# Output stores issued from ScalarE's queue in place of SyncE's, in a residual vector quantizer on one core

## The chip, the cores and the metric

The kernel runs on one core of a Trainium2 chip. The metric is device time in microseconds (us) of one execution, as a median over runs. The engines are named as in the profile: PE (TensorE, matrix products), PEld (its weight loads), DVE (VectorE), ACT (ScalarE), POOL (GpSimd) and SP (SyncE, which here only issues DMAs). "SPq" and "ACTq" are the instruction streams of SP and ACT where they issue DMAs.

## What is computed

The input `x` is 2 x 16000 x 512 in bf16. A three-tap depthwise convolution along time, then SiLU, then four stages of residual quantization with eight code words each, then a second three-tap depthwise convolution over the sum of the chosen words:

```python
z = silu(sum(xp[:, i:i+T, :] * dw_enc[i] for i in range(3)))
res, q = z, 0
for s in range(4):
    cb = codebooks[s]
    d2 = |res|^2 - 2 * res @ cb.T + |cb|^2
    sel = cb[d2.argmin(-1)]
    q = q + sel
    res = res - sel
y = sum(qp[:, i:i+T, :] * dw_dec[i] for i in range(3))
```

The output `y` has the shape and type of `x`, 32.8 MB.

## The kernel before

**Tiling.** The 32000 rows are laid out as 128 partitions by 250 groups. `SIZES` cuts the 250 groups into 17 chunks: 4, 12, fourteen of 16, and 10. Inside a chunk, channels go in four blocks of 128 (index `i`).

**One chunk.** `load` brings `x` in transposed, channels on partitions: for chunks from the third on, `one` (L395) issues one transposing DMA for each group and two for the edges, 18 for a chunk of 16, all on SP, into a tile `XT` of which there are two. `front` forms the convolution: DVE makes three products for each block (L449, tiles `Z` and `T`), of which the first one or two sums run as accumulating DMAs from POOL (L455) and the rest on DVE (L457). ACT does the exponential (L461), the addition of one (L466) and the reciprocal (L162), and DVE multiplies into `RES` (L476). `stage` runs four times: PE scores (L540, L545), DVE takes a maximum (L553, `TR`) and ACT moves the dot products out (L556, `PR`); DVE finds the nearest word in six small steps (L574 to L601); PE turns the one-hot marks (L611), ACT copies them (L618, `OHT`); PE pairs (L626), ACT copies (L631, `OHP`), PE gathers the chosen words (L653, `SEL`) and DVE adds them to `RES` (L659).

**The output.** `finish` calls `outputs` once for every four groups, 64 times in all. There, for each pair of groups, PE decodes into PSUM (L676, tile `Y`) and ACT copies into an SBUF tile `YSB` (L682, 128x1024). After the second pair, `store` (L686) issues one DMA of 512 KB from `YSB` to the output. There are two `YSB` tiles (`YB = 2`), so ACT's copies for the third set of four groups wait until the store of the first has landed.

**What sets the order.** Nothing is scheduled on the chip. `Plan` (L43 to L119) is a list scheduler that runs while the kernel is built: each piece of work is a task with an engine, a time for which it holds that engine, a time after which its result is there, what it needs, a due time, and buffers that it takes and gives (`XT`, `Z`, `T`, `E`, `Y`, PSUM banks and so on). `run` walks through modelled time, gives each free engine the ready task with the earliest due time, and emits its instructions at that moment. Each engine then runs its instructions strictly in the order of emission, and waits on semaphores. `Plan` has lanes that are no engines: the stores were tasks of a lane `OUT` (1.5 held, 3.0 to the result), beside the lane `SP` of the transposes (1.4 held, 2.2 to the result, each one after the one before). So the plan treated stores and transposes as independent of each other, though both were instructions of SP, in order of emission. When PE has nothing ready, `run` may insert a filler product (L350) that keeps its clock up.

**Semaphores of the DMAs.** The framework gives the DMAs of SP and ACT eight semaphores in turn. Each such DMA waits, before it is issued, until the DMA eight places earlier in the order of emission has landed, whichever of the two engines issued that one.

Of the kernel before, what the change touches and what calls it, by code (L numbers as in the profile page):

```python
# [13 lines left out]
ACT = mybir.ActivationFunctionType  # L14
# [108 lines left out]
def kernel(  # L123
# [8 lines left out]
    nc = tc.nc  # L132
# [12 lines left out]
    outv = out.flatten_outer_dims().rearrange("(p g) d -> p g d", g=S)  # L145
# [42 lines left out]
    for i in range(KT):  # L188
# [4 lines left out]
    plan = Plan({"XT": 2, "Z": ZB, "T": TB, "E": EB, "Y": YB, "psG": 2, "psA": 3, "RES": 3, "KEY": 3,  # L193
                 "OH": 3})
# [473 lines left out]
    def outputs(groups, needs, due):  # L668

        u = {}  # L670

        def decode(k):
            Y = u[k] = psA.tile([P, 2, D], F32, name="Y", tag="psa")
            for h, (_, terms) in enumerate(groups[k:k + 2]):
                for a, (lhs, rhs) in enumerate(terms):
                    nc.tensor.matmul(Y[:, h, :], lhsT=lhs(), rhs=rhs, start=(a == 0), stop=(a == len(terms) - 1))  # L676

        def pair(k):
            if k == 0:
                u["YSB"] = ypool.tile([P, J, D], out.dtype, name="YSB")  # L680
            n = len(groups[k:k + 2])
            nc.scalar.activation(u["YSB"][:, k:k + n, :], u[k][:, 0:n, :], ACT.Copy)  # L682

        def store():
            g = groups[0][0]
            nc.sync.dma_start(out=outv[:, g:g + len(groups), :], in_=u["YSB"][:, 0:len(groups), :])  # L686

        c = None
        for k in range(0, len(groups), 2):
            count = sum(len(t) for _, t in groups[k:k + 2])  # L690
            d = plan.add("PE", 0.22 * count, 0.22 * count + 0.2, needs, due, lambda k=k: decode(k), take=("psA",))
            c = plan.add("ACT", 0.93, 1.05, [c, d], due, lambda k=k: pair(k), take=("Y",) if k == 0 else (), give=("psA",))
        plan.add("OUT", 1.5, 3.0, [c], due, store, give=("Y",))

    def edge(name, src, shift):
        t = const.tile([P, P], BF16, name=name)
# [10 lines left out]
    def finish(st, due):  # L707
        A0, A1, A2, A3, B0, B3 = (DEC[k] for k in ("A0", "A1", "A2", "A3", "B0", "B3"))
        g0 = st["g0"]
        for m in range(st["MB"]):  # L710
            g = g0 + m * J
            cur = lambda m=m: st["OHT"][:, m, :]
            prev = kept.get("last")
            needs = [st["turned"], kept.get("turned")] + decoder
            todo = []
            if prev is None:
                FIRST = const.tile([P, P], BF16, name="FIRST")
                kept["first"] = plan.add("DVE", 0.2, 0.3, [st["turned"]], due, lambda cur=cur: nc.vector.tensor_copy(FIRST, cur()))
                kept["FIRST"] = lambda: FIRST
            else:  # L720
                todo.append((g - 1, [(prev, A3), (cur, B3)]))
                todo.append((g, [(cur, A0), (prev, B0)]))
            todo.append((g + 1, [(cur, A1)]))
            todo.append((g + 2, [(cur, A2)]))
            kept["last"] = cur
            if g + J < S:
                outputs(todo, needs, due + 0.02 * m * PERIOD)
                continue
            assert S - 1 == g + 1
            right = plan.add("DVE", 0.5, 0.7, [kept["first"]], due, edge("RIGHT", kept["FIRST"], 1))  # L730
            left = plan.add("DVE", 0.5, 0.7, [st["turned"]], due, edge("LEFT", cur, -1))
            todo[-2] = (S - 1, [(cur, A1), (lambda: kept["RIGHT"], B3)])
            outputs(todo[:-1], needs + [right], due)
            outputs([(0, [(kept["FIRST"], A0), (lambda: kept["LEFT"], DEC["A2LO"])])], needs + [left], due)
        kept["turned"] = st["turned"]
# [41 lines left out]
```

## Time and profile before

| | us |
|---|---|
| median of 3 runs (798.14 to 801.6) | 798.77 |
| time of the profiled execution | 797.84 |
| its span, first to last instruction | 796.1 |
| DVE busy | 672.9 |
| ACT busy | 575.3 |
| PE busy | 565.2 |

How to read it: the profile lists groups of instructions with their line, engine, operation, what they write and read, how many there are, their busy time and mean duration, and the idle time of the engine just before them with what ended it (the releaser). A second view lists waits as "engine line <- releaser: us in total, times, longest us". The queue that SP feeds carried 69.77 MB and took 42.9% of the 16 DMA engines' time, POOL's queue 47.63 MB and 34.6%, and ACT's queue 0.13 MB (three small loads at the start) and 0.1%. The transposes run from 2.5 us to 645 us of the span; 41 of the 64 stores are issued in that time and 23 behind it.

### The profile page before, as it was taken

How to read it: one execution, taken by the hardware profiler on the slowest of the kernel's cores; microseconds unless marked ns; L12 is line 12 of the kernel's file. 1: busy time of each engine (PE TensorE's matmuls, PEld its weight loads, DVE VectorE, ACT ScalarE, POOL GpSimd, SP SyncE). 2: the span in 40 equal slices, each digit the busy share in tenths (PEclk: the TensorE clock that was granted, in tenths of full speed). 3: DMA queues.
4: the chain of work that ended last, by engine and by line, in shares of the span. 5: the costliest groups of instructions: out<-in, count | busy, mean ns of one | idle time of the engine just before them, and what ended most of it. 6: DMA issues, size and time to landing. Idle time of an engine off the chain costs nothing. (4 is left out here: it accounts for less than half of the span.)

```text
span 796.1 us, 24168 instructions
## 1 busy us (share of the span) xinstructions
PE 565.2 (71%) x10688; PEld 323.2 (41%) x10751; DVE 672.9 (85%) x1249; ACT 575.3 (72%) x658; POOL 98.4 (12%) x116
## 2 busy tenths in 40 slices
PE   3036776667667677777786877777774887888885
PEld 3012443244433444343444444444532444454542
DVE  4899688988978998698978999999995999999851
ACT  1519763869489795779779597989684898777454
POOL 1301002010201101010110111011110121100000
PEclk9557799769899999899988999989997899999999
DMA  7614869795999998899996799899989864422133
GB/s 194 113 26 76 164 100 177 143 155 127 169 159 203 201 168 144 175 172 187 138 229 137 132 203 174 172 203 190 193 144 195 145 166 115 114 75 81 55 135 133
DMA packets 167571, 119.08 MB, mean 150 GB/s; under 512 B 146921, under 2 KB 147306, under 8 KB 167338
## 3 DMA queue, kind: packets, MB, share of 16 engines
q1 hardware_dynamic: 153252, 69.77, 42.9%
q0 software_dynamic: 14064, 47.63, 34.6%
q8 instruction: 84, 1.38, 0.7%
q14 instruction: 21, 0.17, 0.1%
q10 hardware_dynamic: 150, 0.13, 0.1%
HBM read 3.70 MB, written 32.77 MB: 46 GB/s over the span
## 5 line engine op out<-in xcount | busy, mean ns | idle before, releaser
L659 DVE TENSOR_TENSOR RES<-RES,SEL 128x2048 bf16<-128x2048 bf16 (+2 forms) x204 | 222.5, 1137 | 29.9 <-PE SEL L653 29.4
L545 PEld LDWEIGHTS <-RES 128*64 128x64 bf16 x8064 | 164.2, 117 | 113.6 <-issue 84.0
L545 PE MATMUL PS<-RES 128*64 128x80 bf16 (+1 forms) x8064 | 189.8, 207 | 21.1 <-DVE RES L476 11.3
L653 PE MATMUL SEL<-OHP,W 64*128 64x512 bf16 (+2 forms) x1224 | 159.3, 393 | 33.6 <-ACT OHP L631 12.6
L455 POOL DMA_DIRECT2D Z<-T x90 | 86.3, 973 | 579.2 <-ACT PR L556 83.4
L682 ACT ACTIVATE YSB<-Y 128x1024 bf16<-128x1024 f32 (+1 forms) x126 | 125.7, 1025 | 31.2 <-DMA out_dram<-YSB 14.6
L461 ACT ACTIVATE E<-Z 128x2048 bf16<-128x2048 bf16 (+2 forms) x68 | 121.5, 1789 | 27.1 <-DVE Z L457 26.0
L553 DVE TENSOR_REDUCE TR<-PS 128x6 bf16<-128x384 f32 (+2 forms) x188 | 95.3, 510 | 30.3 <-PE PS L545 16.9
L162 ACT ACTIVATE E<-E 128x2048 bf16<-128x2048 bf16 (+2 forms) x68 | 119.4, 1787 | 0.2
L556 ACT ACTIVATE PR<-PS 128x48 bf16<-128x48 f32 (+2 forms) x188 | 37.2, 209 | 106.5 <-PE PS L545 68.5
L653 PEld LDWEIGHTS <-W 64*128 64x128 bf16 x1224 | 61.6, 100 | 108.8 <-issue 71.0
L449 DVE TENSOR_SCALAR T<-XT,WENC 128x2048 bf16<-128x2048 bf16 (+2 forms) x136 | 96.5, 717 | 9.5 <-DMA Z<-T 8.7
L676 PE MATMUL Y<-A,OHT 128*128 128x512 bf16 x225 | 79.7, 393 | 20.0 <-ACT YSB L682 7.4
L540 PE MATMUL PS<-MASK,IDENT 128*128 128x384 bf16 (+2 forms) x188 | 61.6, 328 | 44.6 <-ACT PR L556 23.5
L466 ACT ACTIVATE E<-E 128x2048 bf16<-128x2048 bf16 (+2 forms) x51 | 90.9, 1787 | 0.2
L476 DVE TENSOR_TENSOR RES<-Z,E 128x2048 bf16<-128x2048 bf16 (+2 forms) x68 | 77.4, 1140 | 3.4 <-ACT E L162 3.2
L676 PEld LDWEIGHTS <-OHT 128*128 128x128 bf16 x373 | 33.1, 99 | 66.7 <-issue 31.3
L457 DVE TENSOR_TENSOR Z<-Z,T 128x2048 bf16<-128x2048 bf16 (+2 forms) x46 | 46.8, 1018 | 7.7 <-DMA Z<-T 7.7
L611 PE MATMUL ps_oh<-IDENT,OH 128*128 128x128 bf16 x252 | 27.2, 231 | 36.7 <-DVE OH L601 31.0
L449 DVE TENSOR_SCALAR Z<-XT,WENC 128x2048 bf16<-128x2048 bf16 (+2 forms) x68 | 48.4, 714 | 5.6 <-issue 5.3
L350 PE MATMUL PS<-CB,IDENT 128*128 128x512 bf16 x130 | 45.5, 444 | 7.8 <-ACT PR L556 6.3
L618 ACT ACTIVATE OHT<-ps_oh 128x512 bf16<-128x512 bf16 (+2 forms) x68 | 38.2, 566 | 16.1 <-PE ps_oh L611 15.6
(87 smaller groups left out, 389.7 us busy)
## 6 DMA issues: line engine op xcount, KB each, us to landing
Z<-T POOLq DMA_DIRECT2D x84, 512.0 KB, 6.5
out_dram<-YSB SPq DMA_DIRECT2D x61, 512.0 KB, 4.1
XT<-in_x_dram SPq DMA_TRANSPOSE x263, 4.4
Z<-T POOLq DMA_DIRECT2D x6, 384.0 KB, 5.1
RES<-in_x_dram SPq DMA_DIRECT2D x1, 1536.0 KB, 11.2
RES<-in_x_dram SPq DMA_DIRECT2D x1, 640.0 KB, 6.4
W<-in_codebooks_dram POOLq DMA_DIRECT2D x6, 64.0 KB, 5.5
W<-in_codebooks_dram POOLq DMA_DIRECT2D x3, 128.0 KB, 5.2
```

The lines of the kernel that those rows point to most:

```text
L162: nc.scalar.add_instruction(mybir.InstActivation(name=nc.get_next_instruction_name(), engine=mybir.EngineType.Activation, ins=args, outs=[ ...
L449: nc.vector.tensor_scalar(out=places(u[name]), in0=taps(i, k), scalar1=WENC[:, i, k:k + 1], scalar2=None, op0=ALU.mult)
L455: nc.gpsimd.dma_start(out=z, in_=t, accum_op=ALU.add)
L461: nc.scalar.activation(u["E"][:, 0:G, :], u["Z"][:, 0:G, :], ACT.Exp, scale=-1.0)
L466: nc.scalar.activation(e, e, ACT.Copy, bias=1.0)
L476: nc.vector.tensor_tensor(out=st["RES"][:, i, 0:2 * G, LC:LC + HT], in0=halves(u["Z"]), in1=halves(u["E"]), op=ALU.mult)
L545: nc.tensor.matmul(V[h * HT:(h + 1) * HT, r, :], lhsT=half[:, LC:LC + HT], rhs=half[:, lo:hi], start=False, stop=(i == KT - 1), skip_group ...
L553: nc.vector.tensor_reduce(out=u["TR"][:, q:q + m], in_=u["V", q][:, :, own:own + HT], axis=AX.X, op=ALU.max)
L653: nc.tensor.matmul(SEL[:, r, 0:R * HT], lhsT=WORDS[s][k][rows, i * P:(i + 1) * P], rhs=u["OHP"][rows, 0:R * HT], start=(k == 0), stop=(k = ...
L659: nc.vector.tensor_tensor(out=now, in0=now, in1=sel[:, :, 0:G, :], op=ALU.add)
L676: nc.tensor.matmul(Y[:, h, :], lhsT=lhs(), rhs=rhs, start=(a == 0), stop=(a == len(terms) - 1))
L682: nc.scalar.activation(u["YSB"][:, k:k + n, :], u[k][:, 0:n, :], ACT.Copy)
```

## The change

The store becomes an instruction of ACT's stream. In the plan it becomes a task of ACT that holds it for 0.35 and has its result after 3.0; an empty task gives the `YSB` tile back when that result is there.

```diff
         def store():
             g = groups[0][0]
-            nc.sync.dma_start(out=outv[:, g:g + len(groups), :], in_=u["YSB"][:, 0:len(groups), :])
+            nc.scalar.dma_start(out=outv[:, g:g + len(groups), :], in_=u["YSB"][:, 0:len(groups), :])
...
-        plan.add("OUT", 1.5, 3.0, [c], due, store, give=("Y",))
+        sent = plan.add("ACT", 0.35, 3.0, [c], due, store)
+        plan.add("BANK", 0.0, 0.0, [sent], due, lambda: None, give=("Y",))
```

SP then issues three loads at the start and the 264 transposes, and nothing else. Since the plan's costs have changed, the order of the other instructions changes too: ACT's list is the same up to the second store (about 180 us into the span) and differs from there on; those of DVE, PE and POOL differ from about the same place. The instructions are the same ones, apart from six more filler products on PE (156 for 150).

## The prediction

> **What bounds the kernel now.** I read the page's busy times first, then the table of windows, split where the transposes end (645 us), then the waits of each engine.
>
> ```profile
> PE 565.2 (71%) x10688; PEld 323.2 (41%) x10751; DVE 672.9 (85%) x1249; ACT 575.3 (72%) x658; POOL 98.4 (12%) x116
> ```
> ```profile
> core 0: us, PE busy (x) PEld busy (x) DVE busy (x) ACT busy (x) POOL busy (x), PEclk, DMA share, GB/s
> 122.00:645.00 523.00, 382.43 (x7499) 217.86 (x7538) 458.75 (x781) 410.16 (x451) 69.81 (x73) 0.91 0.95 170
> 645.00:796.00 151.00, 123.68 (x2411) 70.19 (x2425) 118.41 (x223) 104.39 (x143) 11.43 (x14) 0.98 0.36 109
> ```
>
> The columns of the second are busy times; the clock and the DMA engines' share stand behind them. In the middle 523 us DVE is busy 88% and ACT 78%, and the DMA engines 95%. DVE comes closest to being the bound, in a fixed order with small waits; the DMA engines have almost no room. After 645 us nothing is full.
>
> What does SP's mixed queue cost today? SP's own waits in that window, then DVE's waits on transposed input, and ACT's on a store:
>
> ```profile
> SPq L686 <- ACT YSB L682: 50.7, 21, 10.3
> ```
> ```profile
> DVE T L449 <- DMA XT<-in_x_dram: 0.8, 1, 0.8
> ...
> DVE Z L449 <- DMA XT<-in_x_dram: 0.2, 1, 0.2
> ```
> ```profile
> ACT YSB L682 <- DMA out_dram<-YSB: 14.6, 5, 10.0
> ```
>
> SP stands before a store that ACT has not filled for 51 us, about 5 us for each chunk, and transposes stand behind it. Yet DVE waited for transposed input only 1.0 us in the whole run. So the transposes are late by some us and nobody notices. What is noticed is a store that lands late: ACT waited 14.6 us for a free YSB, 10.0 of it once. The timelines of SP, ACT and DVE show that one:
>
> ```profile
> 595.28 0.84 SPq L686 DMA_DIRECT2D out_dram<-YSB  x1
> 596.17 7.69 SPq L395 DMA_TRANSPOSE XT<-in_x_dram  x2
> 603.95 3.42 SPq L686 DMA_DIRECT2D out_dram<-YSB  x1
> ```
> ```profile
> 610.70 1.94 ACT L682 ACTIVATE YSB<-Y 128x1024 bf16<-128x1024 f32 x2 [9.99 <-DMA out_dram<-YSB]
> ```
> ```profile
> 612.77 0.56 DVE L553 TENSOR_REDUCE TR<-PS 128x6 bf16<-128x384 f32 x1 [8.87 <-ACT PR L556]
> ```
>
> The store issued at 595.28 landed 15.3 us later, the longest of all; ACT stood 9.99 us, and DVE 8.87 us behind it. Apart from the 1.0 us for XT, it is the one place where SP's queue reaches the engine nearest to the bound.
>
> **The change part by part.** All sums are against the profiled execution's 797.84 us, 0.93 below the median of 798.77; that 0.93 is added at the end.
>
> *Removed from SP: 64 stores and the waits before them.* Worth the 1.0 us that DVE waited for XT. The rest is hidden: the order of DVE's instructions is fixed when the kernel is built, and its products (L449) stand where the plan expects XT, with each transpose 2.2 after the one before, 18 x 2.2 = 40 us for a chunk. The trace's bursts take 36 to 45 us. Earlier transposes find nobody ready. I take -1, between 0 and -1. The transposes still fill the same DMA engines, only up to 5 us sooner in each chunk.
>
> *Added to ACT: 64 DMA issues.* No store on ACT is in the trace, so I bound it. On SP:
>
> ```profile
> L686 SPq DMA_DIRECT2D out_dram<-YSB x64: 332/337/3425, 122.7 to 792.4; - x64
> ```
>
> The 41 before 645 us took 25.1 us together (mean 0.61: half take 0.34, those right behind a transpose 0.52 to 3.42), the 23 after it 7.6 us (0.33 each). ACT's own row is a small load at the start:
>
> ```profile
> L177 ACTq DMA_DIRECT2D TAPS<-in_dw_enc_dram x1: 542/542/542, 0.8 to 0.8; - x1
> ```
>
> That issue lies at 0.77 to 1.31 beside ACT's table load (0.74 to 2.02): ACT's stream issues a DMA while the previous instruction still runs. So an issue costs ACT only what sticks out beyond its predecessor. The new order of ACT's list gives the predecessors: in 11 cases the store's own YSB copy, which must be finished first (nothing hidden: 0.61); in 16 a PR copy of 0.21 (0.40 sticks out); in 10 an OHT copy of 0.57 (0.04); in 27 an OHP copy, another YSB copy or a 1.8 us activation (nothing). 11 x 0.61 + 16 x 0.40 + 10 x 0.04 = 13.5 us of ACT time. Bounds: 0 if all falls into ACT's idle time (113 us of the 523), 33 if nothing is hidden. Of 13.5 I let half reach the end: ACT is idle 22% of the middle, but what waits for ACT, above all PE (23.5 us on PR, 21.9 on OHT, 12.6 on OHP), passes delays on to DVE (29.4 us waiting for SEL). +7.
>
> *A wait moved onto ACT: the semaphores.* A store waits until the DMA eight places earlier in the common order has landed. On SP this was harmless; on ACT, all copies queued behind it would stand, and PE and DVE behind those. In the trace of before, that earlier DMA had landed at least 5.8 us before the store was ready (the store of 231 us) in all 64 cases, and transposes now come sooner, not later. I take 0; each store that did wait would cost up to one transpose's landing, 4.4 us.
>
> *A store behind its neighbours on ACT.* SP issued 0.03 us after the copy when it stood ready. On ACT, one instruction lies between copy and store in 35 cases and two to four in 18: the tile goes out 0.2 to some 4 us later. Behind 24 stores the next instruction is a YSB copy. At the end of the kernel the copies wait for tiles at most 1.4 us. +1.
>
> *The store's DMA on a queue of its own.* Before, a store stood in SP's ring behind up to eight transposes. Landing took a median of 4.3 us while transposes ran and 2.7 after them. On ACT's queue no transposes are ahead of it. I expect two thirds of the 8.87 us stall to go: -6, between -9 and 0 (the engines are 95% busy, and an accumulating transfer issued at 594.90 on POOL's queue also took 15.5 us). The Trainium skill, "DMA: Bandwidth & Descriptors", section "Queues, rings and completion order", says that each DMA engine takes packets from its queues in turn; the trace can't show that yet, since ACT's queue carried 0.1%. The same page, section "Issuing engines are not separate DMA queues", speaks against the gain: all three run on the same 16 engines, and a second issuer saves only issue time. By that this term would be 0 (the third rival).
>
> *A new order.* The plan is made anew from 180 us on. The work is the same; DVE's idle time in the middle is 64 us, and I let a tenth of it, 6 us, fall either way. Six more fillers are planned for PE (156 for 150), a faint sign of more idle time. Value 0.
>
> Sum: 797.84 - 1 + 7 + 0 + 1 - 6 + 0 = 798.8, plus 0.93: about **800 us**.
>
> **The rivals.**
>
> *Stall gone, issue free (788).* Stores land in about 3 us, ACT's waits for tiles vanish, and the issues fall into ACT's idle time: 797.84 - 8.9 - 1 + 0.93 = 789, and 788 with the smaller waits of 0.5 to 1.9 us. For it: DVE's only long wait in the middle is this stall. Against: the DMA engines are full, and 27 of 64 stores have a predecessor too short to hide them.
>
> *ACT queues behind SP's transposes (slower, 812).* If both streams share what turns instructions into descriptors, an ACT store waits for the transpose in work. SP is at transposes for 390 of 523 us, 75%, with a median of 1.39 each; half of one at 75% is 0.52, so 1.13 for each of the 41 stores. With the predecessors in the same shares, 7 x 1.13 + 10 x 0.92 + 6 x 0.56 + 4 x 0.47 + 7 x 0.11 = 23 us stick out, and 2 after 645 us; half of 25 is 13, and with the stall as before 797.84 - 1 + 13 + 1 + 0.93 = 812. It decides once an ACT issue in the middle has a mean above 1 us. For it: SP's stores right behind transposes took up to 3.42. Against: that may be SP's own ring being full.
>
> *The same engines, the same stall (806).* The store lands as late as before, so the -6 is gone: 798.8 + 6 + 0.93, about 806. For it: the transfer on POOL's queue that was as slow.
>
> That the change does nothing (SP free, but nobody waits for SP) is contained in the forecast: it is why the first term is only -1.
>
> **How the numbers follow.** Changes within 0.5% (4 us: 794.8 to 802.8) are about what a measurement of this kernel cannot tell from none. Forecast 0.42, of which 0.30 lies within 4 us and 0.06 on either side, by the new order's 6 us; its own range is 793 to 807. Stall gone 0.22 (0.20 faster, 0.02 same); queueing 0.22 (0.20 slower, 0.02 same); same stall 0.14 (0.10 slower, 0.04 same). Together: faster 0.26, same 0.38, slower 0.36. The range runs from the first rival to a little beyond the second: 788 to 814.
>
> **What would show it.** In the changed profile: ACTq L686 with 64 issues, a median of 0.34 and a mean near 0.6 (above 1: the second rival); no ACT idle time released by an XT transfer in front of a store; landing of stores near 3 us; ACT waits for out_dram below 10 us in all; SP's L686 waits gone and DVE's waits for XT still near 0; DVE busy as before. The forecast is wrong if stores on ACT wait for transposes, if transposes crowd out the accumulating transfers (DVE and ACT now wait 27 us for Z), or if the new order alone moves the time by more than 6 us.

## The result: slower by 7%, and what the profile after shows

The changed kernel took a median of 855.99 us (853.67 to 864.31, 4 runs) against 800.18 us (798.14 to 810.25, 4 runs) for the kernel before on the same chip: a ratio of 1.0725, 95% interval 1.0626 to 1.0824. The forecast was 800 us, with a range of 788 to 814. Some runs of these kernels come out a few per cent longer at a lower granted clock; medians count all runs, and a ratio with its interval compares the others alone. Three readings of the profile after answer to those of before: busy times, the table of windows, and the waits.

The page's busy times, then the windows (the first ends at the same 645 us as before):

```profile
PE 579.2 (68%) x10757; PEld 325.7 (38%) x10757; DVE 671.6 (79%) x1249; ACT 575.9 (68%) x658; POOL 96.8 (11%) x116
```
```profile
core 0: us, PE busy (x) PEld busy (x) DVE busy (x) ACT busy (x) POOL busy (x), PEclk, DMA share, GB/s
122.00:645.00 523.00, 357.30 (x6763) 197.65 (x6762) 411.28 (x704) 368.96 (x409) 63.00 (x67) 0.88 0.81 158
645.00:850.00 205.00, 164.17 (x3162) 93.03 (x3158) 163.53 (x296) 145.66 (x184) 16.68 (x20) 0.95 0.44 109
```

DVE and ACT are busy for as long as before (671.6 and 575.9 us, against 672.9 and 575.3). To these two no work was added, only idle time. (PE's busy time is not compared, since 63 of its 10751 records are missing in the profile before.) In the middle 523 us everything thinned out together: DVE from 88% to 79%, the DMA engines from 95% to 81%, 158 GB/s in place of 170. An engine or a queue that had become the bound would be fuller than before, and none is.

Next, ACT's waits (engine and line, what it waited for, us in total, times, longest). Left out are those for PE and DVE, and for the accumulating DMAs (`Z`):

```profile
ACT YSB L682 <- DMA XT<-in_x_dram: 40.3, 5, 12.4
...
ACT PR L556 <- DMA XT<-in_x_dram: 13.4, 2, 11.6
...
ACT E L461 <- DMA XT<-in_x_dram: 12.1, 2, 7.0
ACT OHT L618 <- DMA XT<-in_x_dram: 9.8, 1, 9.8
...
ACT YSB L682 <- DMA out_dram<-YSB: 4.8, 4, 2.3
...
ACT E L466 <- DMA XT<-in_x_dram: 3.7, 1, 3.7
```

Five of these six rows make no sense as data flow. The copy of decoded output (L682), the copy of scores (L556) and the exponential (L461) read nothing that a transposing DMA writes, and before the change ACT had no such wait at all. Together they are 40.3 + 13.4 + 12.1 + 9.8 + 3.7 = 79.3 us in 11 waits of up to 12.4 us. DVE stands behind them by way of PE and ACT: its wait for `SEL` went from 29.4 to 51.6 us. Before, then after:

```profile
DVE RES L659 <- PE SEL L653: 29.4, 28, 4.7
...
DVE TR L553 <- ACT PR L556: 12.8, 11, 8.9
```

```profile
DVE RES L659 <- PE SEL L653: 51.6, 28, 12.9
...
DVE TR L553 <- ACT PR L556: 22.6, 9, 11.6
...
DVE T L449 <- DMA XT<-in_x_dram: 5.9, 2, 4.6
```

One such wait, followed through the timelines of ACT, SP, PE and DVE (start, us, what; in brackets the idle time before it and its releaser):

```profile
571.21 0.74 ACT L631 ACTIVATE OHP<-ps_pair,NEG 128x512 bf16<-128x512 f32 x1
581.33 0.35 ACTq L686 DMA_DIRECT2D out_dram<-YSB  x1
581.73 0.60 ACT L618 ACTIVATE OHT<-ps_oh 128x512 bf16<-128x512 bf16 x1 [9.78 <-DMA XT<-in_x_dram]
```
```profile
562.41 27.11 SPq L395 DMA_TRANSPOSE XT<-in_x_dram  x18
```
```profile
582.38 4.03 PE L653 MATMUL SEL<-OHP,W 64*128 64x512 bf16 x18 [9.55 <-ACT OHT L618]
```
```profile
583.88 3.78 DVE L659 TENSOR_TENSOR RES<-RES,SEL 128x2048 bf16<-128x2048 bf16 x3 [9.80 <-PE SEL L653]
```

The store's tile was filled at 571.4, and ACT's last instruction ahead of it ended at 571.95. The store was issued at 581.33. In the records of the DMAs, the 11th transpose of the burst that began at 562.41 landed at 581.25, 0.08 us earlier; in the built kernel it is the one that held this store's semaphore last. The trace names the OHT copy as what waited, since that is the next busy instruction; what waited is the store in front of it, and the wait was for a transpose's *semaphore*. PE then stood 9.55 us and DVE 9.80. Of the 64 stores, 13 were issued 0.08 us after the landing of the very transpose that had held their semaphore; in the kernel before, none.

**Why that transpose.** Each DMA of SP and ACT takes the next of eight completion semaphores and waits for the semaphore's previous holder. The turn follows an order that the framework makes when the kernel is built, in which each engine's stream keeps its order. It is *not* the plan's order of emission, as the section on the kernel before has it: in the built kernel before the two differ in 3 of 334 places only, but in the changed kernel in 186. Here is a typical chunk in that order, read from the built kernels (t a transpose, Y a store, | the first transpose of a chunk):

```
before: |tttt Y ttt Y tt Y ttt Y tttttt
after:  |tttttttttttttttttt Y Y Y Y
```

With the stores on SP, SP's own stream kept them between the transposes. On ACT's stream nothing holds them there, and the framework puts the whole burst of 18 ahead of the four stores. Eight places before those stores stand the 11th to 14th transposes of the burst, and the burst cannot start before DVE has released the old `XT`. Counted over the built kernel, 43 stores have a transpose of the running burst eight places ahead, 37 of them the ninth of their chunk's transposes or a later one; before, it was 28, of which 8 were the ninth or later. The semaphores in ACT's list of the built kernel tell the same. Two chunks' stores, by their number in ACT's list:

```
189 L686 DMACopy out_dram<-YSB 128x2048 [waits DMAHW4_49,Activation_49]
197 L686 DMACopy out_dram<-YSB 128x2048 [waits DMAHW5_49,Activation_49]
202 L686 DMACopy out_dram<-YSB 128x2048 [waits DMAHW6_49,Activation_49]
207 L686 DMACopy out_dram<-YSB 128x2048 [waits DMAHW7_49,Activation_49]
234 L686 DMACopy out_dram<-YSB 128x2048 [waits DMAHW0_49,Activation_49]
243 L686 DMACopy out_dram<-YSB 128x2048 [waits DMAHW1_49,Activation_49]
249 L686 DMACopy out_dram<-YSB 128x2048 [waits DMAHW2_49,Activation_49]
257 L686 DMACopy out_dram<-YSB 128x2048 [waits DMAHW3_49,Activation_49]
```

4, 5, 6, 7, then 0, 1, 2, 3: consecutive numbers mean that no transpose lies between a chunk's four stores in the common order. The transposes come ahead of them together: 18 ahead of the first four stores, and 16 between the two groups.

### The profile page after: what moved, and what is told of

The parts are those of the page before. It is cut to its first block, busy times and chain, and to the rows that moved or that the text cites. A ratio compares the mean times of both kernels' runs of the same rounds, so it can differ in the third digit from the quotient of the medians.

```text
span 851.8 us, 24215 instructions
## 1 busy us (share of the span) xinstructions
PE 579.2 (68%) x10757; PEld 325.7 (38%) x10757; DVE 671.6 (79%) x1249; ACT 575.9 (68%) x658; POOL 96.8 (11%) x116
## 4 chain that ended last, share of the span: by engine, by line
DVE 39%; SPq 20%; PE 15%; DMA 11%; ACT 10%; issue 3%; ACTq 1%; POOL 0%; DVEq 0%
SPq L395 20%; DVE RES L659 12%; DMA XT<-in_x_dram 6%; DVE RES L476 5%; DVE TR L553 5%; PE PS L545 5%; PE SEL L653 4%; DVE T L449 4%; ACT YSB L682 3%; PE Y L676 2%; DVE Z L457 2%; DVE Z L449 2%; DMA Z<-T 2%; ACT E L162 2%; ACT E L461 1%
## 5 line engine op out<-in xcount | busy, mean ns | idle before, releaser
L659 DVE TENSOR_TENSOR RES<-RES,SEL 128x2048 bf16<-128x2048 bf16 (+2 forms) x204 | 222.2, 1139 | 52.7 <-PE SEL L653 51.6
L545 PEld LDWEIGHTS <-RES 128*64 128x64 bf16 x8064 | 167.1, 119 | 115.5 <-issue 87.4
L545 PE MATMUL PS<-RES 128*64 128x80 bf16 (+1 forms) x8064 | 192.5, 209 | 17.9 <-DVE RES L476 10.4
L653 PE MATMUL SEL<-OHP,W 64*128 64x512 bf16 (+2 forms) x1224 | 157.2, 388 | 67.2 <-ACT YSB L682 31.2
L682 ACT ACTIVATE YSB<-Y 128x1024 bf16<-128x1024 f32 (+1 forms) x126 | 125.2, 1022 | 63.5 <-DMA XT<-in_x_dram 40.3
L461 ACT ACTIVATE E<-Z 128x2048 bf16<-128x2048 bf16 (+2 forms) x68 | 121.2, 1786 | 37.7 <-DVE Z L457 20.7
L676 PE MATMUL Y<-A,OHT 128*128 128x512 bf16 x249 | 87.6, 399 | 33.1 <-ACT YSB L682 26.2
L556 ACT ACTIVATE PR<-PS 128x48 bf16<-128x48 f32 (+2 forms) x188 | 35.7, 205 | 101.2 <-PE PS L545 47.1
L449 DVE TENSOR_SCALAR T<-XT,WENC 128x2048 bf16<-128x2048 bf16 (+2 forms) x136 | 95.3, 714 | 5.9 <-DMA XT<-in_x_dram 5.9
L676 PEld LDWEIGHTS <-OHT 128*128 128x128 bf16 x373 | 33.7, 100 | 84.3 <-issue 51.6
L350 PE MATMUL PS<-CB,IDENT 128*128 128x512 bf16 x156 | 52.5, 437 | 1.3 <-ACT PR L556 1.3
L676 PE MATMUL Y<-B,OHT 128*128 128x512 bf16 x124 | 49.1, 396 | 6.0 <-ACT OHT L618 4.9
```

Source lines behind the costliest of these rows:

```text
L449: nc.vector.tensor_scalar(out=places(u[name]), in0=taps(i, k), scalar1=WENC[:, i, k:k + 1], scalar2=None, op0=ALU.mult)
L461: nc.scalar.activation(u["E"][:, 0:G, :], u["Z"][:, 0:G, :], ACT.Exp, scale=-1.0)
L545: nc.tensor.matmul(V[h * HT:(h + 1) * HT, r, :], lhsT=half[:, LC:LC + HT], rhs=half[:, lo:hi], start=False, stop=(i == KT - 1), skip_group ...
L653: nc.tensor.matmul(SEL[:, r, 0:R * HT], lhsT=WORDS[s][k][rows, i * P:(i + 1) * P], rhs=u["OHP"][rows, 0:R * HT], start=(k == 0), stop=(k = ...
L659: nc.vector.tensor_tensor(out=now, in0=now, in1=sel[:, :, 0:G, :], op=ALU.add)
```

## The experiments

The theory is that the *order in which the eight semaphores are dealt* costs the time: stores on ACT wait for transposes that they have nothing to do with. Its rivals are the plan's new order of instructions, the queue and the issues on ACT, and the transposes themselves, which freed of the stores run in one burst. The runs are grouped by what they tell apart. Runs of one kernel in one call spread over 10 to 44 us, more than the 0.5% that the prediction took for what can be told, so a ratio with its interval counts for more than a difference of medians.

**The new plan, with the stores on SP.** This leaves out the queue, and with it every wait of ACT for a transpose, and keeps the plan's new costs.

```diff
-            nc.scalar.dma_start(out=outv[...], in_=u["YSB"][...])
+            nc.sync.dma_start(out=outv[...], in_=u["YSB"][...])
```

> The changed plan (store as a task of ACT, 0.35), but the store is issued from SP as before. Three theories share the 56 us. A, shared semaphores: each DMA of SP and ACT waits for the one eight places earlier in the order in which the framework deals eight semaphores; with stores on ACT that order puts a chunk's 18 transposes ahead of its four stores, so ACT stands until about the 11th transpose has landed. B, the new order of the plan. C, the issue on ACT or the store's own queue costs the time itself. A and C expect here 800 (795 to 806) and no ACT idle time ended by an XT transfer; B expects about 856.

Measured: 792.29 us (778.25 to 800.79) against 799.54 for the kernel before. ACT waited for no XT transfer, and for a free `YSB` 5.0 us in place of 14.6 (5.3 in the later call):

```profile
ACT YSB L682 <- DMA out_dram<-YSB: 5.0, 5, 1.9
```

So the new order does not cost the time; it gains a little. In a later call:

> The same plan with the store on SP again (792 in its first runs, from 778 to 801). Between this and the run before only the store's queue differs, and the order of the semaphores is the same. If the queue of its own is worth what SP's mixed queue cost, this is 5 to 15 us slower than that run; if the gain was the new order of the plan, both are alike.

It took 784.29 us against 797.22, ratio 0.9893 (0.9836 to 0.995): a small gain of about 1%. One more thing follows from the line above: the long stall before a free tile went away *with stores still on SP*.

**The queue alone, with the plan of before.** The store is issued by ACT, while the plan keeps it in the lane `OUT`.

```diff
-            nc.sync.dma_start(out=outv[...], in_=u["YSB"][...])
+            nc.scalar.dma_start(out=outv[...], in_=u["YSB"][...])
```

> Only the issuing engine is changed: the plan has its store lane as before, with the same order of all other instructions, and the store is an instruction of ACT. The framework again deals the semaphores with the transposes ahead. A and C expect 840 to 860, with ACT idle time ended by XT transfers of 50 us and more; B expects 800.

Measured: 864.73 us (863.97 to 874.14), ratio 1.0878 (1.0801 to 1.0955). This one line makes the whole loss and more. ACT's waits for XT transfers are 95.3 us, the largest of them:

```profile
ACT PR L556 <- DMA XT<-in_x_dram: 32.1, 3, 12.2
ACT YSB L682 <- DMA XT<-in_x_dram: 26.8, 3, 11.4
ACT E L461 <- DMA XT<-in_x_dram: 23.3, 3, 11.3
ACT OHP L631 <- DMA XT<-in_x_dram: 11.1, 1, 11.1
```

**The semaphores dealt in the plan's order, all else equal.** Each transpose is told to come, in the framework's order, behind the last transpose and the last store that the plan emitted. That is an order at build time, without a wait on the chip. The list of instructions of every engine is the same as in the changed kernel; only which semaphore a DMA takes differs. (Names are shortened here; the last line names the engines of the manual schedule and leaves SP out, whose list comes out the same.)

```diff
+    last = {}
+    def behind(kind, made):
+        if kind == "t":
+            for other in last.values():
+                tc.add_manual_dep(made.ins, other.name, DependencyInfo(NoSync, DATA), reason="order of emission")
+        last[kind] = made.ins
...
-            nc.sync.dma_start_transpose(...)
+            behind("t", nc.sync.dma_start_transpose(...))
...
-            nc.scalar.dma_start(out=..., in_=u["YSB"][...])
+            behind("Y", nc.scalar.dma_start(out=..., in_=u["YSB"][...]))
...
-    with tc.manual_schedule():
+    with tc.manual_schedule(engines={PE, DVE, Activation, Pool}):
```

> The changed kernel with every engine's instructions in the same order, the store on ACT, but the eight semaphores dealt in the plan's order of emission (a transpose may not be placed before a store that the plan emitted earlier; no wait is added on the chip). A store's predecessor is then mostly an old transpose, or one of the first of the burst. A expects most of the 79 us of ACT idle time that an XT transfer ended to go, and 800 to 812. B and C expect about 856 still.

Measured: 781.08 us (772.79 to 787.89), ratio 0.9767 (0.9685 to 0.9849). Again 28 stores have a transpose of the running burst eight places ahead, but only 8 of them the ninth or a later one, and no store was issued at such a landing. The page's busy times, and ACT's one wait for a DMA other than `Z`:

```profile
PE 561.5 (72%) x10697; PEld 324.8 (42%) x10757; DVE 669.9 (86%) x1249; ACT 575.8 (74%) x658; POOL 97.8 (13%) x116
```
```profile
ACT YSB L691 <- DMA out_dram<-YSB: 4.6, 5, 1.3
```

ACT's waits for XT fell from 79.3 us to 0 and the time from 856 to 781 us (in two calls), with the same instructions in the same order on every engine. Twice more, the last time with the changed kernel beside it on one chip:

> The kernel with the semaphores in the plan's order again, for its gain: it was 781 against 799.5 for the kernel before, the runs of both being 15 us and more apart. Expected 775 to 790, and faster than the kernel before by 1 to 3%.

> The changed kernel once more, so that it stands on the same chip as the next two. Theory (false waits through shared semaphores): about 856 us, with about 80 us of ACT idle time ended by XT transfers. Rival (transposes freed of the stores run ahead in one burst and crowd out the other transfers): the same time. It tells nothing apart by itself; it is the reference for the next two.

> The changed kernel with the semaphores dealt in the plan's order. Theory: about 75 us below the changed kernel on the same chip, about 780, and no ACT wait on an XT transfer. Rival (burst of transposes): the gain would have to come from transposes that are held back, so DVE would be found waiting less for Z and the DMA engines' share would be lower than in the changed kernel.

These took 782.34 us (ratio 0.9898, 0.9791 to 1.0005), 859.22 us (1.0767, 1.0648 to 1.0887) and 787.63 us (0.9888, 0.9775 to 1.0001). ACT's waits for XT were 0.3 us in both runs of the plan's order, and 79.7 in the changed kernel. On one chip, the order of the semaphores is worth 859.22 - 787.63 = 71.6 us. The rival of the last two asked for a lower share of the DMA engines once the transposes are held back; in the window from 122 to 645 us of the last run the share is 1.00, against 0.84 in the changed kernel beside it. Here is the window of the last run, then that of the changed kernel:

```profile
122.00:645.00 523.00, 397.31 (x7835) 227.48 (x7835) 472.06 (x803) 422.51 (x469) 73.76 (x80) 0.93 1.00 176
```
```profile
122.00:645.00 523.00, 353.28 (x6644) 196.20 (x6637) 405.48 (x697) 361.68 (x402) 61.74 (x66) 0.87 0.84 153
```

Its other sign, less waiting of DVE for `Z`, points both ways: 18.9 us against 26.1 in this call, but 12.2 against 6.1 in the first profiles of the two kernels. The granted clock differs too, 0.93 against 0.87. In that window it is 0.86 to 0.88 in the three profiles in which ACT stood 79 us and more at stores, and 0.89 to 0.95 in all others, so it went with the waits; how much of the 72 us comes by way of PE's clock was not parted.

The same edit on the queue alone, with the plan of before:

> As the run before (old plan, store on ACT), with the semaphores dealt in the plan's order of emission. A expects 795 to 810; B expects 800; C expects 840 to 860. With the run before, A alone expects a difference of 40 us and more between two kernels whose engines all have the same instructions in the same order.

It took 796.78 us (776.21 to 815.36), ratio 0.9777 (0.9699 to 0.9855): by the medians 68 us below the queue alone, again with the same instruction lists, and again without a wait of ACT for XT. Its waits for a free `YSB` are these:

```profile
ACT YSB L691 <- DMA out_dram<-YSB: 12.0, 7, 4.6
```

**A dose between the two.** Each transpose is ordered only behind the last store *but one*, so that a few more of them come ahead of each store.

> As the run with the semaphores in the plan's order, but a transpose may now be placed one store too early (it must only stand behind the last store but one that the plan emitted). A dose between the two: a store's predecessor is the ninth or a later transpose of the running burst in 8 cases, against 3 in the plan's order and 27 in the changed kernel. The shared-semaphore theory expects a time between them and nearer to the plan's order, 785 to 810, with 5 to 30 us of ACT idle time ended by XT transfers. If something else than these waits parted the two kernels (say, the compiler's treatment of SP's order), it expects 781 again, or 856.

Now 36 stores have a transpose of the running burst eight places ahead, 17 of them the ninth or later. (The expectation has 8, 3 and 27 for this run, the plan's order and the changed kernel; by place among a chunk's 18 transposes they are 17, 8 and 37 in the built kernels.) ACT waited 11.5 us, and 7 stores were issued at such a landing:

```profile
ACT E L472 <- DMA XT<-in_x_dram: 7.4, 1, 7.4
...
ACT E L162 <- DMA XT<-in_x_dram: 4.1, 1, 4.1
```

The time was 796.36 us, ratio 1.0017 (0.9938 to 1.0096), beside 782.34 for the plan's order in the same call: 14 us more by the medians, some 9 by the ratios, for 11.5 us of waits. The two intervals overlap slightly, so by itself this only agrees with the theory.

**Twice the issues.** The plan's order of semaphores, with each store issued as two halves: 126 DMA issues on ACT in place of 64.

```diff
+            for k in range(0, len(groups), 2):
+                n = len(groups[k:k + 2])
+                behind("Y", nc.scalar.dma_start(out=outv[:, g + k:g + k + n, :], in_=u["YSB"][:, k:k + n, :]))
```

> Semaphores in the plan's order, and each store cut in two DMAs of two groups each, issued one behind the other from ACT: 64 more issues on ACT, everything else as there. My forecast charged 64 issues with 13.5 us of ACT time and 7 us at the end; by that, 64 more, which never hide behind their predecessor since that is a DMA issue too, cost 64 x 0.39 = 25 us of ACT time and some 12 us at the end (793). If an issue on ACT costs next to nothing, 781 again (775 to 788).

It took 792.71 us, ratio 0.989 (0.981 to 0.997), against 0.9898 for 64 issues in the same call. The medians differ by 10 us and the ratios not at all, in runs that spread over 33 and 44 us. The cost of 62 more issues is not resolved here; the two intervals together leave room for some 10 us either way, so the 12 us that the prediction's price would give are not clearly excluded.

**The stores on POOL.** This is the other way to part the semaphores: POOL's DMAs have eight of their own. SP holds the transposes alone, as in the change, and runs each chunk's 18 in one burst. The plan is that of before.

```diff
-            nc.sync.dma_start(out=outv[...], in_=u["YSB"][...])
+            nc.gpsimd.dma_start(out=outv[...], in_=u["YSB"][...])
```

> The kernel before with the stores issued by POOL, whose semaphores are not those of SP's transposes. SP holds the transposes alone, as in the change, and each chunk's transposes go in one burst. Theory (false waits on ACT): no ACT wait on an XT transfer, and a time near the kernel before, 785 to 810, the price being what POOL's accumulating DMAs lose behind the stores. Rival (the burst of transposes itself costs the time): 840 or more, as in the change.

It took 796.4 us (786.26 to 808.7), ratio 0.9961 (0.9897 to 1.0025). ACT's waits for DMAs are all here:

```profile
ACT YSB L682 <- DMA out_dram<-YSB: 9.2, 8, 2.7
ACT L461 <- DMA Z<-T: 6.4, 1, 6.4
ACT E L461 <- DMA Z<-T: 3.8, 3, 1.8
```

There is none for XT. Transposes that run in one burst cost nothing that these runs can tell, and the 840 us and more of the last rival did not come. So it falls: what cost the time was ACT standing at the stores.

## Why the prediction was wrong, point by point

**The step that failed** is "A wait moved onto ACT: the semaphores", taken as 0. It measured 71.6 us, from 787.63 to 859.22 on one chip. The prediction had the mechanism, "on ACT, all copies queued behind it would stand, and PE and DVE behind those", and it listed among the signs of error that stores on ACT wait for transposes. What was wrong is the proof that it would not happen. It looked up, for each store, the DMA eight places earlier *in the order of emission*, in the trace of before, and found it landed at least 5.8 us before the store was ready "in all 64 cases". Two things failed in that. The turn of the semaphores follows the framework's order and not the plan's, and that order itself changed when the store left SP's stream. Before the change the two orders were nearly one, so a trace of before could not show it. And the sentence "transposes now come sooner, not later" compared a store with the wrong transpose: each came sooner by up to 5 us, but the one waited for moved from mostly the first eight of a burst (20 of 28) to mostly the 11th to 14th. The price named for such a wait was off as well. "One transpose's landing, 4.4 us" holds if the transpose is already under way; the waits ran to 12.4 us, since SP was still issuing the transposes ahead of it, at 27.11 / 18 = 1.5 us each. The built kernel had shown it: the store's semaphores in ACT's list, 4, 5, 6, 7, 0, 1, 2, 3.

**Removed from SP, -1.** Right in kind. SP's waits at L686 are gone, and the transposes run in one burst. Nobody was waiting for them, as the stores on POOL show, with the same bursts and no gain beyond the spread. (In the changed kernel DVE waited 6.1 us for XT, against 1.0 before.)

**64 issues on ACT, +7.** The price was too high: in the changed kernel an issue took 0.34 us in the median and at most 0.43, not 0.61 in the mean.

```profile
L686 ACTq DMA_DIRECT2D out_dram<-YSB x64: 338/339/431, 121.5 to 848.1; - x64
...
DMA to landing us min/median/max: 2.6/3.4/8.2
```

By the working of the prediction with 0.34, 11 x 0.34 + 16 x 0.13 = 5.8 us would stick out, and half of it is 3. What reaches the end was not resolved.

**The store behind its neighbours, +1,** lies below what the runs can tell.

**The queue of its own, -6.** The stall went, ACT's waits for a free tile falling from 14.6 to 4.8 us, but the queue was not needed for it. With the new plan they are 3.5 to 7.4 us in five profiles without the long false waits, on either queue (5.0 and 5.3 with the stores on SP). With the plan of before they are 12.0 us on ACT with semaphores in order and 9.2 on POOL. So their sum goes mostly with the order of instructions. The one long wait of 10.0 us stands only in the single profile of the kernel before. It is absent with the new plan on SP (the longest is 1.9), and also with the plan of before on ACT (4.6) and on POOL (2.7). Nor do stores land sooner on ACT's queue while transposes run. In the window from 122 to 645 us the median, over the stores whose landing the trace tells, is 4.6, 4.5 and 5.4 us in the three runs of the plan's order of semaphores, and 4.6 in both runs of the new plan on SP. (The changed kernel's 3.9 us was had with the engines at 81%.) The Trainium skill, "DMA: Bandwidth & Descriptors", section "Issuing engines are not separate DMA queues", says just this, that transfers share the same 16 engines whichever engine issues them; these medians agree. The same section says that issuing from several engines saves only sequencer time. For the landing that holds, but what moves with the issue is also the wait in front of it, and that was the whole result.

**The new order, 0 within 6.** It gained 7 us in one call and 13 in another, ratio 0.9893 (0.9836 to 0.995): at or past the edge of the bound.

**The rivals.** "Stall gone" was right about the stall and missed the wait. "ACT queues behind SP's transposes" had the right sign, and its mechanism is refuted: it needed a mean issue above 1 us on ACT, and no issue there took over 0.43. ACT did stand behind SP's transposes, but before the issue and by a semaphore. "The same stall" did not occur.

**Put together,** with the medians of the first experiments: 799.54 before, -7 by the new order (792.29), -11 by queue and issues (781.08; in the later call this step was only 784.29 to 782.34, so it may be nothing), +75 by the dealing of the semaphores (855.99, measured in the call before; 71.6 on one chip). The best version found is the changed kernel with the semaphores in the plan's order: 0.9767, 0.9898 and 0.9888 of the time before in three calls, the last two with intervals that just reach 1. It is not told apart from the new plan with the stores on SP (0.9893), nor from the plan of before with the stores on ACT and the semaphores in order (0.9777).

**What stays open:** how much of the small gain is the queue's and how much the order's, and what an issue on ACT costs at the end; the spread of the runs hides both.

## What to carry to other kernels

A DMA brings a wait to the engine that issues it, and on a compute engine everything queued behind stands with it: before moving one, find out which semaphore it takes and which transfer held that semaphore last, in the *built* changed kernel and not in the trace of before. Where a trace shows a compute instruction waiting for a DMA whose data it does not read, look at the DMA issue just ahead of it in the same stream: it is a false wait through a shared semaphore, and it goes when the semaphores are dealt in the order in which the work really happens, or when the two kinds of DMA have semaphores of their own. Identical instruction lists on every engine do not mean identical kernels; these two were 72 us apart.

## What the hardware showed that was not expected

- A DMA issue on ACT had a steady price where issues stand apart: 0.338 us in the median and at most 0.431 over the changed kernel's 64, in the same stretch in which SP issued transposes at 1.27 us each. With two issues one behind the other the median stayed, but 11 of 126 took 0.9 us and more:

```profile
L697 ACTq DMA_DIRECT2D out_dram<-YSB x126: 338/339/2142, 122.2 to 775.2; - x126
```

- On SP, right behind transposes, the 512 KB store took up to 3.42 us before the change, and 1.34 with the new plan on SP:

```profile
L686 SPq DMA_DIRECT2D out_dram<-YSB x64: 332/338/1342, 124.0 to 789.2; - x64
```

- On POOL the same store's issue took 0.56 us in the median and up to 1.02. It landed in a median of 5.3 us in the window from 122 to 645 us, though POOL's queue carried the accumulating DMAs as well.
- With the DMA engines' share at 0.96 to 1.03 in that window, it made no difference beyond the spread which of the three queues carried the stores: medians to landing of 4.6 us on SP, 4.5 to 5.7 on ACT and 5.3 on POOL.
- From the landing of the transpose that held the semaphore to the issue of the store that waited for it, 0.08 us passed, in all 13 such stores of the changed kernel.
